# Attention over inducing points and a PReLU layer on one core: how the first batch is loaded and cast

## The chip, the cores and the metric

The kernel runs on one core of a Trainium2 chip. The metric is the device time of one execution in microseconds (us): the median of the runs given. Everything shown below of a profile is of one profiled execution, whose times are counted from the start of its span.

## The reference

`x` has 4 batches of 12480 rows of 128 numbers, `inducing` is 32x128. For each batch

```python
def mab(q, kv):
    s = (q @ kv.T) / sqrt(128)
    a = softmax(s)              # with 1e-9 added to the sum
    return a @ kv
h   = mab(inducing, x)          # 32 x 128, needs all of the batch's x
y   = mab(x, h)                 # 12480 x 128
hid = y @ w_in                  # 128 -> 2048
out = (maximum(hid, 0) + alpha * minimum(hid, 0)) @ w_out   # 2048 -> 128
```

All inputs and the output are f32 in device memory. So a batch has a first stage, which needs the whole batch and gives `h`, and a second one, which is work per row.

## The kernel before

**Tiles.** A batch is cut into six blocks of 2048 rows (16 tiles of 128 rows, one 128x2048 tile `xs` in f32 or `xn` in bf16) and a rest of 192 rows (`xn_left`). For the first batch `first_pieces` numbers them: piece 0 is block 0, piece 1 the rest, pieces 2 to 5 are blocks 1 to 4, pieces 6 and 7 are the two halves of block 5.

**First stage, for the first batch (the ramp).** Each piece is loaded as bf16 by a DMA that casts on its way (`a_load_cast`, L276 and L281, issued by POOL). Then TensorE transposes it in parts (`t` steps, L325), ScalarE or VectorE copy the parts out of the accumulators into `xT` (`c` steps, L331 and L333; a part is cut 0, 1 or 2 of a piece: 8, 4 and 4 tiles), TensorE multiplies by the inducing points (`s`, L340), VectorE takes the running minimum (`m`, L354 and L363), ScalarE the exponentials (`e`, L379, and the factors `f`, L397), TensorE transposes those (`u`, L417), they are copied out (`v`), TensorE multiplies them by `xn` (`h`, L434) and VectorE adds the result to a running sum (`g`, L448 and L450). A tail of small steps (`mg` to `hT`, L469 to L548) makes `h` of it.

What each engine does in the ramp is written out by hand in one string, `order`; each engine works through its own steps of it in that order. In a step the digit is the piece, the digit after the point the part, the last letter the engine (`a` ScalarE, `v` VectorE). `W4` means four matmuls on a tile of zeros (`warm`, L925, 512 columns each), whose result nobody reads.

**Second stage.** Its weights are loaded by POOL's queue too, behind the pieces: `w_in` cast to bf16 (`w_in_b`), `w_out` in f32. `w_in` is transposed by a DMA of SP's queue (`winT`, L1048). POOL multiplies `w_out` by `1 - alpha` (`weights`, tile `W`, L943) and by `alpha` (`linear_weights`, tile `AW`, L952), four instructions of 128x512 each; of the latter two come with the `weights` and two later, behind POOL's copy of `rep` (L1068). The work per row is then done in 416 visits: a visit multiplies four sets of 128 hidden units by 512 rows (L765), ScalarE or VectorE apply the relu (tile `gt`, L778 and L780), and one visit later TensorE multiplies by `W` (L791) into an accumulator, which is copied out (`ob`, L837, L844, L846) and stored by SP's queue. Four visits finish 512 rows, 16 visits a block.

**What else is in the visits.** The first stage of the next batch, and the softmax of the rows that come next, are laid into the visits by `at(visit, step)`. For batch 1 the pieces are loaded in f32 by SP (`a_load`, L290, into one of the four buffers of `xs_pool`), cast by POOL (`a_cast`, L308) and transposed by a DMA of SP's queue (`xT<-xn`, L317). The softmax of the rows of block 1 is in the list `when`: scores, maximum, difference (POOL, L683), exponential (ScalarE, L645), sums (POOL, L669), reciprocal (VectorE, L706), product (POOL, tile `rep`, L714) and a DMA transpose (`a<-rep`, L723). A planner (`Plan`) chooses for each relu and copy whether ScalarE or VectorE does it, from costs that are written in the code, before the program is built.

SP issues its DMAs in the order in which they stand. Each waits for the data that it needs, and for the DMA that held its completion semaphore before it (there are eight).

Of the kernel before, what the change touches and what calls it, by code (L numbers as in the profile page):

```python
# [21 lines left out]
P = 128  # L22
R = 4
ST = 16
# [6 lines left out]
def kernel(  # L31
# [9 lines left out]
    nc = tc.nc  # L41
# [3 lines left out]
    B, N, C = x.shape  # L45
# [218 lines left out]
        eng.memset(st.da[:], 0.0)  # L264
        return st

    def a_load_cast(st, pc):


        r0, nt, last = supers[pc.s]  # L270
        if pc.full:
            if pc.s not in st.xn:
                st.xn[pc.s] = xn_pool.tile([P, ST, C], bf16, name="xn", tag="xn")
            rows = x[st.b, r0 : r0 + nt * P, :].rearrange("(p j) c -> p j c", p=P)
            ts = slice(pc.t0, pc.t0 + pc.n)
            nc.gpsimd.dma_start(out=st.xn[pc.s][:, ts], in_=rows[:, ts])  # L276
        else:
            st.xn[pc.s] = xn_left
            for t in range(nt):
                n = last if t == nt - 1 else P  # L280
                nc.gpsimd.dma_start(  # L281
                    out=xn_left[:n, t, :], in_=x[st.b, r0 + t * P : r0 + t * P + n, :]
                )

    def a_load(st, pc):
        s = pc.s
        r0, nt, last = supers[s]
        if pc.full:
            st.xs[s] = xs_pool.tile([P, ST, C], f32, name="xs", tag="xs")
            nc.sync.dma_start(  # L290
                out=st.xs[s][:],
                in_=x[st.b, r0 : r0 + nt * P, :].rearrange("(p j) c -> p j c", p=P),
            )
        else:
            st.xs[s] = xs_left
            for t in range(nt):
                n = last if t == nt - 1 else P
                nc.sync.dma_start(
                    out=xs_left[:n, t, :], in_=x[st.b, r0 + t * P : r0 + t * P + n, :]
                )  # L300

    def a_cast(st, pc):
        s = pc.s
        r0, nt, last = supers[s]
        xs = st.xs[s]
        if pc.full:
            st.xn[s] = xn_pool.tile([P, ST, C], bf16, name="xn", tag="xn")
            nc.gpsimd.tensor_copy(out=st.xn[s][:], in_=xs[:])  # L308
        else:
            st.xn[s] = xn_left  # L310
            for t in range(nt):
                n = last if t == nt - 1 else P
                nc.gpsimd.tensor_copy(out=xn_left[:n, t, :], in_=xs[:n, t, :])

    def a_turn(st, pc):
        s, nt = pc.s, pc.n
# [544 lines left out]

    xn_left = const.tile([P, supers[-1][1], C], bf16, name="xn_left")
    e1T_left = const.tile([P, supers[-1][1] * P], bf16, name="e1T_left")
    blank = const.tile([P, 512], bf16, name="blank")
    for t in (xn_left, blank, e1T_left):
        nc.vector.memset(t[:], 0.0)
    st = new_state(0)
    for pc in first_pieces[:2]:
        a_load_cast(st, pc)
    ident32 = const.tile([P, P], f32, name="ident32")  # L870
    make_identity(nc, ident32[:])
    ind_f = const.tile([M, C], f32, name="ind_f")
# [9 lines left out]
    xs_left = const.tile([P, supers[-1][1], C], f32, name="xs_left")  # L882
    for pc in first_pieces[2:]:
        a_load_cast(st, pc)
# [36 lines left out]
    def warm(n):  # L921

        ps = sums(0)
        for _ in range(n):
            nc.tensor.matmul(ps[:], blank[:, :P], blank[:], start=True, stop=True)  # L925
# [12 lines left out]

    a2s = {}

    def weights(i, eng):
        ks = slice(i * R, (i + 1) * R)
        eng.tensor_tensor(  # L943
            out=W1[:, ks, :],
            in0=w_out_f[:, ks, :],
            in1=om_al[:, ks].unsqueeze(2).broadcast_to([P, R, C]),
            op=MULT,
        )

    def linear_weights(i):  # L950
        ks = slice(i * R, (i + 1) * R)
        nc.gpsimd.tensor_tensor(  # L952
            out=AW[:, ks, :],
            in0=w_out_f[:, ks, :],
            in1=alT[:, ks].unsqueeze(2).broadcast_to([P, R, C]),
            op=MULT,
        )
# [12 lines left out]
    kept = {}  # L970

    def first_products():
        b_products(st, 0, 0, BT)
# [5 lines left out]
    def first_less():  # L979
        kept["be"] = new_e()  # L980
        b_less(kept["b"], 0, BT, kept["bm"], kept["be"])

    def begin(step):


        if step[0] == "W":
            warm(int(step[1:]))
            return
        plain = {
            "mg": lambda: a_max(st),  # L990
            "rb": lambda: kept.update(rb=a_factors_pe(st)),
            "mm": lambda: a_factors_min(st, kept["rb"]),
            "mf": lambda: a_factors_exp(st),
            "ex": lambda: a_worth(st),
            "dn": lambda: a_total(st),
            "pd": lambda: kept.update(pd=a_den_pe(st)),
            "rec": lambda: a_den_rec(st, kept["pd"]),
            "ph": lambda: kept.update(ph=a_sum_pe(st)),
            "hT": lambda: a_sum_div(st, kept["ph"]),
            "b": first_products,  # L1000
            "bm": first_most,
            "bs": first_less,
            "be": lambda: b_exp_once(kept["be"], BT, w0[:, :BT]),
            "bt": lambda: kept.update(bt=b_turn_pe(w0[:, :BT], BT)),
            "ba": lambda: b_turn_copy(st, 0, 0, BT, kept["bt"], False),
            "b2": lambda: b_products(st, 0, BT, ST - BT, later),
            "w": lambda: a_w(st),
            "hw": lambda: a_w_copy(st),
            "hwv": lambda: a_w_copy(st, False),
        }  # L1010
        if step in plain:
            plain[step]()
            return
        f, act = step[0], step[-1] == "a"
        p, _, part = step[1:].rstrip("av").partition(".")
        pc = first_pieces[int(p)]
        if f in "tc":
            t0, n = cuts[pc.n][int(part)]
            if f == "t":
                kept["t", p, part] = a_turn_pe(st, pc, t0, n)  # L1020
            else:
                a_turn_copy(st, pc, t0, n, kept.pop(("t", p, part)), act)
        elif f == "u":
# [43 lines left out]
    def first_turn_dma():  # L1067
# [6 lines left out]
        for i in range(NV // 2, NV):  # L1074
            linear_weights(i)

    def first_sum():
        src = b_tree(w0, ST)
# [83 lines left out]
    for b in range(B - 1):  # L1162
# [90 lines left out]
```

## Time and profile before

| | |
|---|---|
| median of 3 runs (lowest, highest) | 601.41 us (600.49, 602.48) |
| time of the profiled execution | 601.52 us |
| its span, first to last instruction | 599.4 us |
| mean granted TensorE clock | 0.993 |
| PE, ACT, DVE, POOL busy | 98%, 91%, 87%, 36% of the span |
| first product of a visit (L765) starts at | 31.46 us |

The span is 2.1 us shorter than the execution's time; what lies around it is taken as fixed. The ramp is what stands ahead of 31.46 us, 5% of the span; the visits and the last stores take the rest.

### The profile page before, as it was taken

Reading aid. Unit: us, or ns where it says so; the run is one execution under the profiler, and the core shown is the slowest. Engines: PE = TensorE matmul, PEld = TensorE weight load, DVE = VectorE, ACT = ScalarE, POOL = GpSimd, SP = SyncE. Lnnn points to the kernel's source line nnn. Section 1 sums busy time; section 2 is a strip of 40 time slices with the busy share of each in tenths; the row PEclk is TensorE's granted clock in tenths of the full one; section 3 lists DMA queues with packets and bytes.
Section 4 is the critical chain, followed back from the end, with each engine's and each line's share of the span. In section 5 each row is a group of like instructions: output and inputs, shape, how many; then the busy total and the mean of one; then the engine's idle time right before and its main releaser. Section 6 shows DMA issues by size and latency. Waiting matters only on the chain.

```text
span 599.4 us, 22670 instructions
## 1 busy us (share of the span) xinstructions
PE 586.0 (98%) x9439; PEld 437.7 (73%) x9441; DVE 519.1 (87%) x944; ACT 546.8 (91%) x1110; POOL 214.3 (36%) x255
## 2 busy tenths in 40 slices
PE   7899999999999999999999999999999999999997
PEld 3567777777777777777777777777777777777775
DVE  5778988888998899988898889988899899899986
ACT  4679999999999999999999999999999999999996
POOL 4176535303416436233136155233133134144010
PEclk9899999999999999999999999999999999999999
DMA  8947999544178797641256999931242231442311
GB/s 163 212 149 158 211 199 221 106 91 73 55 188 188 224 221 177 108 99 54 73 127 204 189 197 238 169 81 55 72 77 68 73 90 54 115 74 68 90 57 58
DMA packets 122088, 76.81 MB, mean 128 GB/s; under 512 B 103953, under 2 KB 106113, under 8 KB 119681
## 3 DMA queue, kind: packets, MB, share of 16 engines
q1 hardware_dynamic: 120112, 70.50, 52.0%
q0 software_dynamic: 1648, 4.77, 4.0%
q8 instruction: 74, 1.21, 0.9%
q14 instruction: 30, 0.24, 0.2%
q10 hardware_dynamic: 224, 0.09, 0.1%
HBM read 28.07 MB, written 25.56 MB: 89 GB/s over the span
## 4 chain that ended last, share of the span: by engine, by line
PE 93%; DMA 4%; ACT 1%; issue 0%; DVE 0%; DVEq 0%; SPq 0%; ACTq 0%; POOLq 0%
PE bp L791 64%; PE hh L765 22%; DMA xn<-in_x_dram 3%; PE bp L818 2%; PE hh L601 2%; PE hh L434 1%; PE hh L340 1%; DMA a<-rep 1%; ACT gt L778 1%; PE hh L559 0%; PE hh L417 0%; PE bp L925 0%; DVEq L1248 0%; PE hh L325 0%; PE hh L482 0%
## 5 line engine op out<-in xcount | busy, mean ns | idle before, releaser
L778 ACT ACTIVATE gt<-hh 128x512 bf16<-128x512 f32 x887 | 471.1, 606 | 29.4 <-PE hh L765 20.5
L780 DVE TENSOR_SCALAR gt<-hh 128x512 bf16<-128x512 f32 x673 | 435.4, 685 | 51.3 <-PE hh L765 41.1
L791 PE MATMUL bp<-W,gt 128*128 128x128 bf16 x6240 | 416.6, 220 | 0.2 <-DVE gt L780 0.2
L791 PEld LDWEIGHTS <-gt 128*128 128x128 bf16 x6240 | 349.4, 98 | 85.7 <-issue 79.1
L765 PE MATMUL hh<-a,HW 32*128 32x512 bf16 (+2 forms) x1664 | 159.3, 371 | 1.9 <-ACT gt L778 1.3
L714 POOL TENSOR_TENSOR rep<-e,rc 128x2048 bf16<-128x2048 f32 (+1 forms) x24 | 84.5, 3520 | 19.1 <-DVE rc L706 19.1
L683 POOL TENSOR_TENSOR e<-e,smx 128x512 f32<-128x512 f32 (+1 forms) x24 | 24.6, 1025 | 169.9 <-DVE smx L678 169.9
L765 PEld LDWEIGHTS <-HW 32*128 32x128 bf16 x1664 | 41.0, 91 | 43.8 <-issue 7.3
L669 POOL TENSOR_TENSOR t<-e 128x256 f32<-128x256 f32 (+1 forms) x24 | 17.2, 716 | 131.3 <-ACT e L645 131.3
L844 ACT COPY ob<-bp 128x512 f32<-128x512 f32 (+1 forms) x63 | 37.1, 589 | 2.3 <-PE bp L791 1.4
L308 POOL CAST xn<-xs 128x2048 bf16<-128x2048 f32 x18 | 34.0, 1888 | 6.4 <-DMA xs<-in_x_dram 5.8
L669 POOL TENSOR_TENSOR t<-t 128x128 f32<-128x128 f32 (+3 forms) x100 | 30.3, 303 | 7.8
L354 DVE TENSOR_SCALAR_CACHE_REDUCE s<-hh 128x512 f32<-128x512 f32 (+2 forms) x29 | 18.1, 623 | 6.2 <-PE hh L340 5.9
L846 DVE COPY ob<-bp 128x512 f32<-128x512 f32 x31 | 21.1, 680 | 0.0
L379 ACT ACTIVATE e1T<-s,rm 128x512 bf16<-128x512 f32 (+1 forms) x25 | 17.7, 706 | 2.5 <-DVE rm L363 2.5
L818 PEld LDWEIGHTS <-a 32*128 32x128 bf16 x392 | 14.9, 93 | 6.3 <-issue 0.9
L818 PE MATMUL bp<-HA,a 32*128 32x128 bf16 x392 | 19.3, 215 | 0.0
L645 ACT ACTIVATE e<-e 128x512 f32<-128x512 f32 (+1 forms) x24 | 14.8, 615 | 1.3 <-POOL e L683 1.3
L678 DVE TENSOR_REDUCE smx<-e 128x16 f32<-128x512 f32 (+1 forms) x24 | 15.9, 662 | 0.0
L601 PE MATMUL hh<-hT,xT 128*128 128x32 bf16 x372 | 13.0, 177 | 0.4 <-DVE hT L548 0.4
L601 PEld LDWEIGHTS <-xT 128*128 128x128 bf16 x384 | 12.3, 96 | 0.9 <-issue 0.9
L659 ACT COPY e<-hh 128x512 f32<-128x512 f32 (+1 forms) x19 | 10.9, 573 | 2.0 <-PE hh L601 1.1
(110 smaller groups left out, 182.0 us busy)
## 6 DMA issues: line engine op xcount, KB each, us to landing
out_dram<-ob SPq DMA_DIRECT2D x97, 256.0 KB, 2.6
xs<-in_x_dram SPq DMA_DIRECT2D x18, 1024.0 KB, 5.9
xn<-in_x_dram POOLq DMA_DIRECT2D x5, 512.0 KB, 7.9
w_out_f<-in_moe_w_out_dram POOLq DMA_DIRECT2D x1, 1024.0 KB, 19.6
xn<-in_x_dram POOLq DMA_DIRECT2D x2, 256.0 KB, 14.0
w_in_b<-in_moe_w_in_dram POOLq DMA_DIRECT2D x1, 512.0 KB, 16.3
a<-rep SPq DMA_TRANSPOSE x25, 4.6
xT<-xn SPq DMA_TRANSPOSE x18, 6.2
```

What stands on the lines that cost most here:

```text
L308: nc.gpsimd.tensor_copy(out=st.xn[s][:], in_=xs[:])
L601: nc.tensor.matmul(ps[w, t, :], st.xT[:, tile0[s] + t, w], hTs[b][:], start=True, stop=True)
L669: nc.gpsimd.tensor_tensor(out=t[:, :n], in0=src[:, :n, :w], in1=src[:, :n, w : 2 * w], op=ADD)
L683: nc.gpsimd.tensor_tensor(out=st.e2[s][:, :n], in0=st.e2[s][:, :n], in1=st.m2[s][:, :n].unsqueeze(2).broadcast_to([P, n, M]), op=SUB,)
L714: nc.gpsimd.tensor_tensor(out=rep[:, :n], in0=st.e2[s][:, :n].unsqueeze(2).broadcast_to([P, n, R, M]), in1=rc[:, :n].unsqueeze(2).unsqueez ...
L765: nc.tensor.matmul(hh[:, q * cols + w.start : q * cols + w.stop], HWs[b][rows, v * P : (v + 1) * P], a2[rows, t0 : t0 + nt, :].rearrange(" ...
L778: nc.scalar.activation(out=gt[:, :cols], in_=hh[:, :cols], func=RELU)
L780: nc.vector.tensor_relu(gt[:, :cols], hh[:, :cols])
L791: nc.tensor.matmul(blk.acc[:, t * C : (t + 1) * C], gt[:, (q * nt + t) * P : (q * nt + t + 1) * P], W1[:, k, :], start=(not blk.begun), st ...
L818: nc.tensor.matmul(blk.acc[w, t * C : (t + 1) * C], blk.a2[rows, blk.t0 + t, w], HAs[b][rows, :], start=(not blk.begun and t == 0), stop=F ...
L844: nc.scalar.copy(out=ob[:, :nt], in_=acc)
L846: nc.vector.tensor_copy(out=ob[:, :nt], in_=acc)
```

## The change

- The ramp's pieces are loaded as f32 by SP's queue (`a_load`), five of them at the start. The others, `w_in` and `w_out`, are loaded by `load_next`: one after the last cast of each of blocks 0, 1, 2 and 3, whose buffers of `xs_pool` they take.
- The pieces are cast to bf16 in the parts in which they are transposed (`a_cast_part`, steps `k`), by POOL (`p`), ScalarE (`a`) or VectorE (`v`): thirteen part casts by POOL, and piece 1, five by ScalarE, one by VectorE. `w_in` is cast by POOL as a whole (`kwp`).
- `W` steps have 256 columns instead of 512, and there are more of them.
- `order` is written anew. The first four tiles' softmax no longer waits for the copy of `HW`, which ScalarE makes (`hw`) instead of VectorE (`hwv`).
- POOL makes three of the four `AW` products ahead of its copy of `rep`, one behind it.
- In the visits, `first_rec` comes one visit later, some steps of block 1's softmax one or two later, and the cast, transpose, scores and so on of batch 1's first two pieces four later.

```diff
-    def a_load_cast(st, pc):
...
-            nc.gpsimd.dma_start(out=st.xn[pc.s][:, ts], in_=rows[:, ts])
...
     def a_load(st, pc):
...
+            if s not in st.xs:
+                st.xs[s] = xs_pool.tile([P, ST, C], f32, name="xs", tag="xs")
+            rows = x[st.b, r0 : r0 + nt * P, :].rearrange("(p j) c -> p j c", p=P)
+            ts = slice(pc.t0, pc.t0 + pc.n)
+            nc.sync.dma_start(out=st.xs[s][:, ts], in_=rows[:, ts])
...
+    def a_cast_part(st, pc, t0, n, eng):
+        s = pc.s
+        if not pc.full:
+            a_cast(st, pc)
+            return
+        if s not in st.xn:
+            st.xn[s] = xn_pool.tile([P, ST, C], bf16, name="xn", tag="xn")
+        ts = slice(pc.t0 + t0, pc.t0 + t0 + n)
+        to, of = st.xn[s][:, ts], st.xs[s][:, ts]
+        if eng == "a":
+            nc.scalar.copy(out=to, in_=of)
+        else:
+            (nc.gpsimd if eng == "p" else nc.vector).tensor_copy(out=to, in_=of)
...
-    blank = const.tile([P, 512], bf16, name="blank")
+    blank = const.tile([P, 2 * P], bf16, name="blank")
...
-    for pc in first_pieces[:2]:
-        a_load_cast(st, pc)
+    for pc in first_pieces[:5]:
+        a_load(st, pc)
...
-    nc.gpsimd.dma_start(out=w_in_b[:], in_=moe_w_in)
-    w_out_f = xs_pool.tile([P, NK, C], f32, name="w_out_f", tag="xs")
-    nc.gpsimd.dma_start(out=w_out_f[:], in_=moe_w_out.rearrange("(k p) c -> p k c", p=P))
...
-    warm(7)
+    warm(14)
...
-    warm(4)
+    warm(9)
...
+    def load_next(done):
+        if not waiting:
+            return
+        what = waiting.pop(0)
+        if what == "w_in":
+            kept["w_in"] = xs_pool.tile([C, DFF], f32, name="w_in_f", tag="xs")
+            nc.sync.dma_start(out=kept["w_in"][:], in_=moe_w_in)
+        elif what == "w_out":
+            kept["w_out"] = xs_pool.tile([P, NK, C], f32, name="w_out_f", tag="xs")
+            nc.sync.dma_start(
+                out=kept["w_out"][:], in_=moe_w_out.rearrange("(k p) c -> p k c", p=P)
+            )
+        else:
+            for pc in what:
+                a_load(st, pc)
...
-        t0.1 t0.2 c0.2v t0.0 c0.0v c0.1a s0 t1.0 t2.0 m0 t2.2 c1.0v e0 t2.1 c2.2v c2.0v
-        s1 m1 e1 W4 t3.2 t3.0 f1 c3.2a c2.1v t3.1 c3.1a s2 u0 c3.0v u1 s3 v0a v1a t4.0
-        t4.1 m2 e2 t4.2 h0 h1 m3 c4.0v f3 c4.2a f2 c4.1v u2 g0 s4 g1 t5.2 v2v e3 c5.2a
-        t5.1 t5.0 c5.1a u3 m4 e4 c5.0v v3a t6.1 c6.1v h2 s5 t6.0 t7.1 g2 m5 t7.0 c6.0a
-        c7.1a c7.0v s6 m6 u4 h3 v4v e5 s7 e6 f4 m7 u5 u6 ex v5v h4 h5 mg g3 e7 rb f5 f6
-        u7 v6v g4 dn h6 mm v7a g5 mf h7 g6 f7 pd g7 rec ph hT W1 b w bm bs hwv b2 be W1
-        bt ba W2
+        k1.0p k0.2p k0.1p t0.2 k0.0v t0.0 c0.2v k2.1p k3.0p k3.2p t0.1 c0.0v c0.1v k2.2a
+        W8 t2.2 k2.0a k4.0p s0 t1.0 c2.2a c1.0a m0 W6 s1 t2.1 t2.0 k4.1p k3.1a m1 c2.1v
+        e0 t3.1 c2.0v c3.1v e1 W1 t3.0 c3.0a t3.2 f1 c3.2v k4.2a s2 W4 s3 m2 u0 u1 k5.0p
+        e2 k5.2p t4.2 m3 c4.2v t4.0 v0a v1a t4.1 u2 c4.0v h0 c4.1a v2v g0 f2 h1 k5.1a
+        k6.0p W2 s4 W1 t5.0 t5.2 t5.1 k6.1p k7.0p g1 e3 k7.1p m4 c5.0v f3 u3 c5.2a t6.0
+        c5.1v W3 s5 e4 t6.1 u4 v3a c6.0v m5 t7.0 c6.1a t7.1 v4a s6 f5 c7.0v h2 kwp c7.1v
+        W2 s7 m6 m7 e5 e6 mg h3 g2 f6 W2 u5 v5v f4 h4 u6 g3 rb e7 h5 u7 v6v h6 g4 ex mm
+        g5 f7 v7a W2 h7 mf dn pd g6 g7 rec W2 ph hT W3 b w bm bs be b2 W4 bt ba hw W5
...
+    waiting = [first_pieces[5:6], first_pieces[6:], "w_in", "w_out"]
...
-            for i in range(NV // 2):
+            for i in range(NV - 1):
                 linear_weights(i)
...
-    at(6, first_rec, cost=[("v", 160)])
+    at(7, first_rec, cost=[("v", 160)])
...
-            when = [1, 2, 3, 4, 5, 7, 8, 11]
+            when = [1, 2, 3, 5, 6, 9, 9, 11]
...
-            m = n + (8 * (p - 1) if p > 1 else p)
+            m = n + (8 * (p - 1) if p > 1 else p if b else p + 4)
```

More of the change, by code (lines that the diff above doesn't have):

```diff
@@ L265, in new_state @@
         return st
-    def a_load_cast(st, pc):
[L270 to L275, printed above, removed]
-            nc.gpsimd.dma_start(out=st.xn[pc.s][:, ts], in_=rows[:, ts])
[L277 to L283, printed above, removed]
     def a_load(st, pc):
@@ L288, in a_load @@
         if pc.full:
[L289 to L293, printed above, removed]
+            if s not in st.xs:
[3 more added lines that the diff above has]
+            nc.sync.dma_start(out=st.xs[s][:, ts], in_=rows[:, ts])
         else:
@@ L867 @@
     st = new_state(0)
-    for pc in first_pieces[:2]:
-        a_load_cast(st, pc)
+    xs_left = const.tile([P, supers[-1][1], C], f32, name="xs_left")
+    for pc in first_pieces[:5]:
+        a_load(st, pc)
     ident32 = const.tile([P, P], f32, name="ident32")
@@ L924, in warm @@
         for _ in range(n):
-            nc.tensor.matmul(ps[:], blank[:, :P], blank[:], start=True, stop=True)
-    warm(7)
+            nc.tensor.matmul(ps[:, : 2 * P], blank[:, :P], blank[:], start=True, stop=True)
+    warm(14)
     itp = ring([C, M], bf16)
@@ L939 @@
     a2s = {}
+    kept = {}
     def weights(i, eng):
@@ L944, in weights @@
             out=W1[:, ks, :],
-            in0=w_out_f[:, ks, :],
+            in0=kept["w_out"][:, ks, :],
             in1=om_al[:, ks].unsqueeze(2).broadcast_to([P, R, C]),
@@ L953, in linear_weights @@
             out=AW[:, ks, :],
-            in0=w_out_f[:, ks, :],
+            in0=kept["w_out"][:, ks, :],
             in1=alT[:, ks].unsqueeze(2).broadcast_to([P, R, C]),
@@ L1007, in begin @@
             "w": lambda: a_w(st),
+            "kwp": lambda: nc.gpsimd.tensor_copy(out=w_in_b[:], in_=kept["w_in"][:]),
             "hw": lambda: a_w_copy(st),
@@ L1014, in begin @@
         f, act = step[0], step[-1] == "a"
-        p, _, part = step[1:].rstrip("av").partition(".")
+        p, _, part = step[1:].rstrip("avp").partition(".")
         pc = first_pieces[int(p)]
@@ L1022, in begin @@
                 a_turn_copy(st, pc, t0, n, kept.pop(("t", p, part)), act)
+        elif f == "k":
+            a_cast_part(st, pc, *cuts[pc.n][int(part)], step[-1])
+            done = first_pieces[int(p)].s
+            if pc.full and step == last_cast[done]:
+                load_next(done)
         elif f == "u":
@@ L1036 @@
     order = """
-        t0.1 t0.2 c0.2v t0.0 c0.0v c0.1a s0 t1.0 t2.0 m0 t2.2 c1.0v e0 t2.1 c2.2v c2.0v
-        s1 m1 e1 W4 t3.2 t3.0 f1 c3.2a c2.1v t3.1 c3.1a s2 u0 c3.0v u1 s3 v0a v1a t4.0
-        t4.1 m2 e2 t4.2 h0 h1 m3 c4.0v f3 c4.2a f2 c4.1v u2 g0 s4 g1 t5.2 v2v e3 c5.2a
-        t5.1 t5.0 c5.1a u3 m4 e4 c5.0v v3a t6.1 c6.1v h2 s5 t6.0 t7.1 g2 m5 t7.0 c6.0a
-        c7.1a c7.0v s6 m6 u4 h3 v4v e5 s7 e6 f4 m7 u5 u6 ex v5v h4 h5 mg g3 e7 rb f5 f6
-        u7 v6v g4 dn h6 mm v7a g5 mf h7 g6 f7 pd g7 rec ph hT W1 b w bm bs hwv b2 be W1
-        bt ba W2
-    """
+        k1.0p k0.2p k0.1p t0.2 k0.0v t0.0 c0.2v k2.1p k3.0p k3.2p t0.1 c0.0v c0.1v k2.2a
[6 more added lines that the diff above has]
+        g5 f7 v7a W2 h7 mf dn pd g6 g7 rec W2 ph hT W3 b w bm bs be b2 W4 bt ba hw W5
+    """
+    waiting = [first_pieces[5:6], first_pieces[6:], "w_in", "w_out"]
+    last_cast = {}
+    for step in order.split():
+        if step[0] == "k" and step != "kwp":
+            last_cast[first_pieces[int(step[1])].s] = step
     for step in order.split():
@@ L1073, in first_turn_dma @@
         )
-        for i in range(NV // 2, NV):
-            linear_weights(i)
+        linear_weights(NV - 1)
     def first_sum():
```

4 lines of the change are left out of this document (removed).

## The prediction, made before the changed kernel ran

> **What bounds the kernel now.** First the page's chain of waits, then the same chain in order of time:
>
> ```profile
> PE 93%; DMA 4%; ACT 1%; issue 0%; DVE 0%; DVEq 0%; SPq 0%; ACTq 0%; POOLq 0%
> ```
>
> ```profile
> 1.25 5.33 DMA xn<-in_x_dram
> ...
> 6.86 14.41 DMA xn<-in_x_dram
> 21.32 1.03 PE hh L325 x8
> ```
>
> From 31.4 us on the chain is TensorE's own work, and no relayout of the ramp shortens that. Ahead of it, up to 21.3 us, the chain is the loads. The timeline shows how the pieces arrive and what follows the last:
>
> ```profile
> 9.64 1.07 PE L325 MATMUL hh<-ident,xn 128*128 128x128 bf16 x16 [0.55 <-DMA xn<-in_x_dram]
> 12.10 1.07 PE L325 MATMUL hh<-ident,xn 128*128 128x128 bf16 x16 [0.24 <-DMA xn<-in_x_dram]
> 14.56 1.07 PE L325 MATMUL hh<-ident,xn 128*128 128x128 bf16 x16 [0.29 <-DMA xn<-in_x_dram]
> 17.07 1.07 PE L325 MATMUL hh<-ident,xn 128*128 128x128 bf16 x16 [0.34 <-DMA xn<-in_x_dram]
> ...
> 21.32 1.03 PE L325 MATMUL hh<-ident,xn 128*128 128x128 bf16 x8 [0.66 <-DMA xn<-in_x_dram]
> ...
> 31.46 0.61 PE L765 MATMUL hh<-a,HW 32*128 32x512 bf16 x6
> ```
>
> Pieces 2 to 5 come 2.47 us apart (1.05 MB read each), piece 7 at 21.3; the visits start 9.1 us after its transposes end at 22.35. Eight transposes there take as long as sixteen before. The table by stretches says why:
>
> ```profile
> core 0: us, PE busy (x) PEld busy (x) DVE busy (x) ACT busy (x) POOL busy (x), PEclk, DMA share, GB/s
> 7.00:17.00 10.00, 7.71 (x111) 5.11 (x109) 7.74 (x24) 6.28 (x17) 2.11 (x3) 1.00 1.06 205
> 17.90:21.20 3.30, 1.74 (x37) 1.03 (x34) 2.22 (x6) 2.36 (x6) 0.00 (x0) 1.00 1.09 204
> 21.30:24.60 3.30, 3.28 (x42) 2.23 (x42) 1.88 (x8) 2.08 (x6) 0.00 (x0) 0.50 1.02 297
> 28.10:31.40 3.30, 3.06 (x39) 1.17 (x38) 1.83 (x5) 0.31 (x1) 3.30 (x4) 0.50 0.92 313
> 29.60:32.00 2.40, 2.40 (x25) 0.60 (x25) 0.81 (x3) 0.12 (x2) 2.40 (x4) 0.60 0.96 396
> ```
>
> In two stretches of the ramp the granted clock is half, each behind a stretch with a half-idle TensorE. The last row is one f32 load by SP's queue (batch 1's first) alone on the DMA engines: 396 GB/s, so 2.65 us for 1.05 MB. In the early visits one wait stands out:
>
> ```profile
> 40.46 0.63 ACT L645 ACTIVATE e<-e 128x512 f32<-128x512 f32 x1 [1.25 <-POOL e L683]
> 41.62 0.39 PE L765 MATMUL hh<-a,HW 32*128 32x512 bf16 x2 [0.84 <-ACT gt L778]
> ```
>
> POOL made two `AW` products (2.03 us, from 37.38) ahead of that difference; ScalarE stood behind it, and TensorE behind ScalarE's relus.
>
> **Part 1, the loads.** SP has nothing to wait for at the start; ScalarE's first DMA is issued at 0.75, so I take 0.7 for SP's. That first DMA, of 16 KB, lands 1.6 us after its issue. With 2.65 of data piece 0 lands at 0.7+1.6+2.65=5.0 (before: 6.6). The other bound is the least of the f32 loads' own landings, 5.2 after issue: 5.9. Piece 1 (96 KB) adds 0.25. Then four whole pieces and two halves, five times 2.65: pieces 2 to 7 land at 7.9, 10.5, 13.2, 15.8, 17.2 and 18.5, `w_in` at 21.1, `w_out` at 23.8. The later ones wait for casts: piece 5's load for piece 0's, done by 7, while the queue has data until 13.2; piece 6's for piece 2's, done by 9.5; `w_in`'s by 12. None of these waits ends last. Piece 7 gains 21.3-18.5=2.8 us.
>
> **Part 2, the casts.** POOL's 128x2048 cast takes 1.89 us, its 128x128 one 0.29; a line through both gives 0.61 for 512 and 1.04 for 1024. Piece 7 needs two in a row, ready at 18.5+1.22=19.75. POOL has 10 casts of 512, three of 1024 and piece 1's two (0.59): 9.8 us between 5 and 19.75, so it keeps up. ScalarE and VectorE are closer. ScalarE from piece 2's first part to the last copy of piece 6: ten 512-copies at 0.55 (0.59 in a row of two takes 1.13), two of 1024 taken as 1.0, two of 256 at 0.33, four exponentials at 0.74, a small one at 0.45, three factors at 0.2: 12.2 us, from 7.9 to 20.1, against 20.0 by the loads. VectorE by the same counting has 11.7 us from 5.0. Both are covered if they hardly wait; no rows show ScalarE or VectorE casting f32 from SBUF in this shape, and I take their PSUM copies' durations. VectorE's one cast (0.66 at that rate, 1.2 at half) is done before piece 2 lands, and costs nothing either way. The last transposes then end at 20.3, with 0.5 us for eight at full clock, against 22.35: 2.05 us gained.
>
> The page SBUF — State Buffer of the Trainium skill (section Who interferes with whom) says that POOL and VectorE block each other for a whole instruction when VectorE runs a copy or cast in its two-port mode, which would speak against casting on POOL. Here POOL's eight products of 128x512 took 1.033 to 1.039 us with VectorE's copies beside some and not others, and its 18 casts 1.881 to 1.891; only the one new SBUF cast of VectorE is of a kind that no row shows, and by the rule it would hold POOL for its 0.66 us, at piece 0.
>
> **Part 3, the clock and the tail.** `W` steps are added where TensorE waited: eight matmuls of 256 columns between the last transposes and `hT`, and twelve behind. I take the clock as full. That shortens what is TensorE's in the tail: the chain's five groups from 22.35 to 24.74 (2.38 us, about half of it array time, of which VectorE's and ScalarE's steps then hide most) 0.4; `rep`'s transposes 0.62 to 0.41 (the same sixteen at 35.79) 0.2; the last `W`, 1.03 us ahead of the first visit, to 0.54: 0.4, as the copy `a` was done at 31.03. The `hwv` copy leaves VectorE, whose `ba` waited for TensorE anyway: nothing. Sum 1.0. `W` (four at 1.04) starts at 23.8 and `AW` ends at 31.0; the first is needed at 30: hidden. The visits start at 31.46-2.05-1.0=28.4.
>
> A rule of the Trainium skill (TensorE: Matmul & The Clock Gate, Part 1) halves the clock after an idle window of about 3.4 us; by its words the added matmuls would buy nothing, as no wait was that long, and the sum would lack the 1.5 us of clock in Parts 2 and 3: 599.8. This trace disagrees: the longest wait of 17.9 to 21.2 was 1.2 us, and the clock halved.
>
> **Part 4, the early visits.** One `AW` product instead of two ahead of the difference, and the exponential a visit later: 0.84 of TensorE's wait and some 0.2 around it go. Against that, batch 1's first scores, maxima and `e` transposes now fall on visits 16 to 21, where block 1's outputs begin and `xs`'s next load stands in SP's queue. A VectorE step of 0.68 in the wrong place costs TensorE that much; the trace has no such row, so between 0 and two of them, 1.4. I take 0.8. SP's queue: block 2's `a<-rep` held TensorE for 0.40 us at 82.18, since a DMA transpose behind a load takes SP 5.6 to 6.3 us (1.9 otherwise). The small `e1T_left` transpose now stands behind that load, the large one behind it, and the load comes about a visit earlier: 0.4 as before, up to 2 if not. Net gain 0.2.
>
> **Sum.** 601.5 (its own execution; 0.1 above the median) less 3.05 and 0.2: 598.3.
>
> **Rivals.** (a) *The clock halves all the same.* For: full activity is not shown by any row for the new order. Against: `order` has 45 `W` matmuls of 256 columns where it had 8 of 512. Price: the 0.5 of Part 2, the 1.0 of Part 3 and 0.3 around them, 600.1. (b) *The three engines wait for each other.* ScalarE is busy 6.28 of 10.0 us and 2.36 of 3.3 (72%) in the two stretches above; in the changed ramp it needs nearly 100%. At 85% its 12.2 us take 14.4, the last copy comes 2.2 later, 600.5; at 72% they take 16.9, 4.8 later: 603.1. From 79% down it is slower than before. (c) *F32 to f32 loads at the pace of before's only one in the ramp, `w_out`*: `winT` was issued at 23.68, when `w_in` had landed, `W` started at 27.68, 4.0 us for 1.05 MB, 3.87 without the lead. Piece 7 then lands at 5.0+0.25+19.4=24.6, 6.1 later than in my sum: 604.4, slower. It decides above 3.3 us a piece (319 GB/s). Against it stands the 396 GB/s row; that row had the DMA engines to itself, as the new ramp has. (d) *Better*: the casting loads' 2.47 us also holds here (0.9) and Part 4 costs nothing (0.8): 596.6.
>
> **How the numbers follow.** The forecast has 0.62, its own range 597.0 to 599.5. (a) 0.10, (b) 0.14, (c) 0.08, (d) 0.06. The measurement tells 0.3%, 1.8 us, from no change. Faster: forecast, (d) and 0.04 of (b), 0.72. Same: (a) and 0.06 of (b), 0.16. Slower: (c) and 0.04 of (b), 0.12. The range goes from (d) to just above (a) and the middle of (b), 596.6 to 600.9.
>
> **What would show it.** In the changed profile: sixteen transposes about 2.65 us apart, the last at about 20 behind POOL's casts; granted clock 1.00 from 18 to 31; ScalarE over 90% busy from 8 to 20; first L765 near 28.4; no wait over 0.5 us behind `e` of L645; `a<-rep` at block 2 within 0.5 us. Transposes 3.3 us or more apart would make (c) right, loads done early with ScalarE's queue late (b), half clock (a). If the visits start at 28.4 and the time is not under 599.6, Part 4 was wrong.

## The result, and the profile after

| | before | changed |
|---|---|---|
| median (lowest, highest), 14 runs each, same chip | 601.23 us (599.39, 602.48) | 603.67 us (601.96, 605.32) |
| time of the profiled execution, its span | 601.52, 599.4 us | 601.96, 600.0 us |
| first product of a visit starts at | 31.46 us | 29.88 us |
| from there to the start of the last visit | 561.45 us | 563.78 us |

The changed kernel is slower: ratio 1.0042, 95% interval 1.0030 to 1.0054. Its profiled execution is its quickest one, 1.7 us under the median; so the trace below shows it at its best, and what it lacks is looked for in the experiments.

The page's chain of waits has hardly changed, since the visits carry it:

```profile
PE 93%; DMA 3%; ACT 1%; POOL 1%; issue 0%; DVE 0%; DVEq 0%; ACTq 0%
```

The same chain in order of time, up to the first pieces (start, length, what):

```profile
1.20 5.27 DMA al_f<-in_moe_alpha_dram
6.60 0.26 PE hh L923
6.86 2.03 PE bp L916 x9
8.89 1.40 PE hh L321 x16
10.29 0.87 PE bp L916 x8
```

The loads of `x` have left the chain. In their place stands an 8 KB load of ScalarE's queue (`alpha`, landed at 6.47 us instead of 2.81, now that the loads of `x` are issued ahead of it), and behind it TensorE never waits again until 24 us: part of what holds it there are the fillers (L916), nine of them for 2.03 us at half clock.

TensorE's timeline, with the transposes of pieces 4 and 5, the last part of piece 6, piece 7, and the first visit:

```profile
16.13 1.07 PE L321 MATMUL hh<-ident,xn 128*128 128x128 bf16 x16
18.58 1.06 PE L321 MATMUL hh<-ident,xn 128*128 128x128 bf16 x16
...
20.96 0.40 PE L321 MATMUL hh<-ident,xn 128*128 128x128 bf16 x4
...
21.41 0.73 PE L321 MATMUL hh<-ident,xn 128*128 128x128 bf16 x8
...
29.88 0.60 PE L761 MATMUL hh<-a,HW 32*128 32x512 bf16 x6
```

The last transposes end at 22.14 us; before it was 22.35. From there to the first visit it is 7.74 us, before 9.11. POOL's timeline shows what stands between the last data and those transposes:

```profile
16.82 1.60 POOL L309 CAST xn<-xs 128x1024 bf16<-128x1024 f32 x2 [0.91 <-DMA xs<-in_x_dram]
19.24 2.44 POOL L309 CAST xn<-xs 128x512 bf16<-128x512 f32 x4 [0.83 <-DMA xs<-in_x_dram]
```

Piece 6 landed at 19.19, piece 7 at 20.46 (before 21.27). Piece 6's two casts end as piece 7 lands, piece 7's start at 20.5 and end at 21.68, so POOL held nothing up here. The table by stretches, the same ones as before:

```profile
core 0: us, PE busy (x) PEld busy (x) DVE busy (x) ACT busy (x) POOL busy (x), PEclk, DMA share, GB/s
7.00:17.00 10.00, 9.99 (x113) 7.85 (x112) 8.19 (x23) 6.79 (x15) 5.40 (x10) 1.00 1.01 417
17.90:21.20 3.30, 3.27 (x43) 2.18 (x43) 2.95 (x10) 3.30 (x10) 2.37 (x5) 1.00 1.01 415
21.30:24.60 3.30, 3.30 (x82) 2.42 (x79) 3.09 (x14) 3.14 (x11) 1.88 (x2) 1.00 1.00 288
28.10:31.40 3.30, 2.84 (x50) 1.42 (x47) 1.76 (x6) 1.88 (x5) 3.30 (x4) 1.00 0.93 278
```

The clock is full from 18 us on, the loads move 415 to 417 GB/s, and TensorE is busy without a gap. Ahead of visit 7 the wait that stood out is gone (ScalarE's exponential, now at L641, follows two relus without a wait); visit 7 starts 3.45 us after visit 6 before, 2.22 us after. But TensorE's own waits from visit 6 to the end of block 2 (engine, line, releaser: us in total, times, longest) are now

```profile
PE hh L761 <- DMA a<-rep: 1.6, 1, 1.6
PE hh L336 <- DMA xT<-xn: 0.9, 1, 0.9
PE hh L336 <- DVE hs L446: 0.4, 1, 0.4
```

The starts of visits, changed less before, tell the story in one line: visit 0 -1.58, visit 7 -2.81, visit 15 -3.14, visit 16 -1.66, visit 23 -0.24, visit 31 +0.81, visit 36 +0.64, last +0.74. All of it, and more, is given back between visits 15 and 31. POOL and SP's queue say how:

```profile
46.32 3.61 POOL L710 TENSOR_TENSOR rep<-e,rc 128x2048 bf16<-128x2048 f32 x1 [3.39 <-PE hh L597]
49.88 1.89 POOL L290 CAST xn<-xs 128x2048 bf16<-128x2048 f32 x1
51.71 0.53 POOL L295 CAST xn_left<-xs_left 128x128 bf16<-128x128 f32 x2
```

```profile
49.96 1.82 SPq L719 DMA_TRANSPOSE a<-rep  x1
51.87 3.72 SPq L313 DMA_TRANSPOSE xT<-xn  x1
55.69 1.20 SPq L313 DMA_TRANSPOSE xT<-xn_left  x1
56.94 0.57 SPq L275 DMA_DIRECT2D xs<-in_x_dram  x1
58.08 5.55 SPq L313 DMA_TRANSPOSE xT<-xn  x1
```

POOL idles 3.39 us ahead of block 1's product. The row names a product of TensorE that ended then; what POOL needs is VectorE's reciprocal, which now comes at visit 9 and ends at 46.18 us; the cast of batch 1's first piece, which used to lie ahead of the product, comes behind it. So `rep` and the two transposes of `xT` reach SP's queue together: `a<-rep` lands 6.1 us after its issue (before 4.5), visit 16 waits 1.60 us for it, and behind these the next load and the next transpose are late too: 0.86 us at 67.3.

### The profile page after: what moved, and what is told of

Its sections match the earlier page's. It is cut to its first block, busy times and chain, and to the rows that moved or that the text cites. A ratio compares the mean times of both kernels' runs of the same rounds, so it can differ in the third digit from the quotient of the medians.

```text
span 600.0 us, 22789 instructions
## 1 busy us (share of the span) xinstructions
PE 589.0 (98%) x9490; PEld 442.5 (74%) x9490; DVE 520.1 (87%) x945; ACT 549.5 (92%) x1115; POOL 218.9 (36%) x260
## 4 chain that ended last, share of the span: by engine, by line
PE 93%; DMA 3%; ACT 1%; POOL 1%; issue 0%; DVE 0%; DVEq 0%; ACTq 0%
PE bp L787 62%; PE hh L761 21%; PE bp L814 2%; PE hh L597 2%; DMA xT<-xn 2%; PE hh L336 1%; PE hh L430 1%; PE bp L916 1%; PE hh L321 1%; DMA a<-rep 1%; DMA al_f<-in_moe_alpha_dram 1%; ACT gt L774 1%; POOL rep L710 1%; PE hh L413 0%; PE hh L555 0%
## 5 line engine op out<-in xcount | busy, mean ns | idle before, releaser
L814 PEld LDWEIGHTS <-a 32*128 32x128 bf16 x392 | 14.9, 93 | 6.7 <-issue 1.6
L641 ACT ACTIVATE e<-e 128x512 f32<-128x512 f32 (+1 forms) x24 | 14.8, 617 | 0.0
L916 PE MATMUL bp<-blank 128*128 128x256 bf16 x68 | 12.5, 323 | 1.2 <-DVE blank L862 1.2
```

The lines of the kernel that those rows point to most:

```text
L814: nc.tensor.matmul(blk.acc[w, t * C : (t + 1) * C], blk.a2[rows, blk.t0 + t, w], HAs[b][rows, :], start=(not blk.begun and t == 0), stop=F ...
```

## The experiments

Each kernel ran beside the kernel before on one chip, 12 times (e5 9, e6 7, e7 10 and e14 6 times). The four groups e1 to e4, e5 to e8, e9 to e12 and e13 to e15 ran on different chips, where the kernel before had medians of 601.18, 600.80, 600.97 and 600.97 us. "Visits" is the time from the first to the last visit's start less that of before (561.45 us), from the one profiled execution.

| kernel | median (range) us | ratio to before, 95% | visit 0 at | visits |
|---|---|---|---|---|
| e1_ramp_only | 601.91 (599.61–603.94) | 0.9997–1.0024 | 29.90 | +0.56 |
| e2_visits_only | 603.30 (600.51–605.94) | 1.0017–1.0055 | 31.37 | +3.48 |
| e3_pieces_back | 599.95 (598.81–601.95) | 0.9968–1.0003 | 31.68 | +0.08 |
| e4_rec_back | 600.74 (599.96–602.30) | 0.9991–1.0014 | 32.07 | +0.47 |
| e5_no_head_W | 603.71 (603.02–607.19) | 1.0026–1.0065 | 31.83 | +2.04 |
| e6_no_W | 603.86 (603.45–607.23) | 1.0033–1.0076 | 31.77 | +5.79 |
| e7_cast_loads | 602.14 (601.72–603.28) | 1.0000–1.0031 | 29.14 | +2.87 |
| e8_rec_pieces | 600.49 (599.45–602.33) | 0.9974–1.0004 | 29.91 | -0.43 |
| e9_cast_best | 599.51 (598.78–602.67) | 0.9959–0.9995 | 29.74 | +0.05 |
| e10_cast_no_W | 600.89 (600.09–606.27) | 0.9985–1.0029 | 31.10 | +5.10 |
| e11_before_early | 600.35 (599.12–601.30) | 0.9971–1.0002 | 30.62 | -0.59 |
| e12_cast_pieces | 598.89 (597.42–603.27) | 0.9944–0.9984 | 30.61 | -1.49 |
| e13_warm_first | 601.05 (598.74–603.22) | 0.9989–1.0016 | 31.08 | -0.01 |
| e14_after_warm_first | 604.46 (603.27–605.75) | 1.0045–1.0079 | 31.95 | +2.57 |
| e15_cast_no_nine | 598.83 (597.72–601.17) | 0.9960–0.9982 | 30.11 | -1.72 |

The profiled executions of e4, e6 and e10 are the longest of their runs, so their last two columns are not typical.

### The ramp alone, the visits alone, and each visit edit undone

e1 is the changed kernel with all three edits of the visits undone; e2 is the kernel before with only these:

```diff
-    at(6, first_rec, cost=[("v", 160)])
+    at(7, first_rec, cost=[("v", 160)])
-            when = [1, 2, 3, 4, 5, 7, 8, 11]
+            when = [1, 2, 3, 5, 6, 9, 9, 11]
-            m = n + (8 * (p - 1) if p > 1 else p)
+            m = n + (8 * (p - 1) if p > 1 else p if b else p + 4)
```

e3 undoes the last of the three only, in the changed kernel; e4 has `[1, 2, 3, 5, 6, 8, 8, 11]` there instead; e8 is both.

> The changed kernel with the steps in the visits put back where they were (first_rec at 6, block 1's list as before, batch 1's first two pieces not moved). Theory (the time is lost in visits 15 to 36, because the moved steps pile DMA transposes up in SP's queue): the ramp's 1.6 us and about 1 us of the early wait stay won, nothing is given back: 598 to 599.5 us, ratio 0.995 to 0.997, no wait of TensorE for a<-rep over 0.5 us. Rival (any earlier start of the visits runs into loads and transposes that can't come earlier): the gain is given back by visit 36, 600.5 to 602.

> The kernel before with only the moved steps in the visits (first_rec at 7, block 1's new list, batch 1's first two pieces four visits later). Theory: the early wait of 0.84 us behind POOL goes, then 2 to 4 us are lost in visits 15 to 36: 602.5 to 604.5. Rival (the ramp's earlier end is what makes the transposes late): 600 to 601.5, no loss.

> The changed kernel with batch 1's first two pieces back at their visits, block 1's new list kept. Theory: block 1's a<-rep still comes late (its reciprocal is at visit 9, and now two transposes of SP's queue may stand ahead of it), 1.5 to 3 us lost at visit 16; the later waits, up to visit 31, go: 601 to 603. Rival: all of the loss is the moved pieces': 598 to 599.5.

> The changed kernel with block 1's reciprocal and product at visit 8 instead of 9, all else as changed. Theory: rep is ready about 1.5 us earlier, the wait of 1.6 us for a<-rep at visit 16 shrinks under 0.5, part of it comes back at visit 22 and after (pieces' transposes wait behind the load): 602 to 603.3. Rival (the transposes of the pieces alone make it late, by sharing the DMA engines): no change from 603.7.

> The changed kernel with two of the visits' edits undone: batch 1's first two pieces four visits earlier, as before, and the reciprocal and product of block 1's softmax at visit 8 instead of 9. Kept are the third AW product ahead of rep, the first softmax's reciprocal a visit later, and the difference, exponential and sums' new visits. Theory: undoing the first alone gave 599.95 and the second alone 600.74; each takes away another wait behind visit 15 (the transposes of batch 1's first piece behind a load, and block 1's a behind VectorE's reciprocal), so both together keep the early visits' gain of 1.2 us and the ramp's: 598.3 to 599.8, faster than before by 0.2 to 0.5%. Rival (both are one queue's crowding, and either cure is enough): 599.7 to 600.8, no better than the better one alone.

The visits' edits alone cost 2.1 us (603.30 against 601.18 of their group), and either of two cures takes the loss away: pieces back 3.7 us of the changed kernel's median, reciprocal a visit earlier 2.9. Both together gain 3.2, no more than one alone: of e8's theories the rival held. So by the medians the two edits cost only together. (The medians of e3 and e4 came out below the ranges of their theories, that of e1 above its own.) In e1 POOL has the cast again where the changed kernel has its wait:

```profile
43.03 1.89 POOL L290 CAST xn<-xs 128x2048 bf16<-128x2048 f32 x1
44.86 0.53 POOL L295 CAST xn_left<-xs_left 128x128 bf16<-128x128 f32 x2
45.35 3.60 POOL L710 TENSOR_TENSOR rep<-e,rc 128x2048 bf16<-128x2048 f32 x1
```

and in e3, with the reciprocal still late, SP's queue has done the transposes of `xT` ahead of `a<-rep`, 4.6 us apart from it:

```profile
44.09 1.93 SPq L313 DMA_TRANSPOSE xT<-xn  x1
47.19 1.17 SPq L313 DMA_TRANSPOSE xT<-xn_left  x1
51.76 2.00 SPq L719 DMA_TRANSPOSE a<-rep  x1
```

The wait of 1.6 us for `a<-rep` at visit 16 is gone there. It is not gone in e1, which has the old visits: its `rep` is done at 48.95, but SP is busy with `xT<-xn_left` until 49.2 and with two output stores until 50.3. So the ramp alone came out at 601.91, no different from before, though in its profile the visits start 1.56 us earlier; how much of that is this wait was not tried by itself.

### The fillers

e5 leaves out `warm(9)` and the order's first `W8`, `W6`, `W1` and `W4`; e6 leaves out every `W` of the order:

```diff
-        W8 t2.2 k2.0a k4.0p s0 t1.0 c2.2a c1.0a m0 W6 s1 t2.1 t2.0 k4.1p k3.1a m1 c2.1v
+        t2.2 k2.0a k4.0p s0 t1.0 c2.2a c1.0a m0 s1 t2.1 t2.0 k4.1p k3.1a m1 c2.1v
```

> The changed kernel without the fillers between its first transposes: W8, W6, W1 and W4 of the order and the nine matmuls behind the transpose of alpha are left out; the later W steps stay. Theory: TensorE is busy without a gap from 6.8 to 24 us in the changed ramp, much of it at half clock, so these fillers stand on its path: without them TensorE waits for casts and loads again in the first pieces, piece 2's first transposes start up to 1 us earlier, the visits start at 29.0 to 30.0 whatever the clock does at the start, and the median is 601.5 to 603.0, up to 2 us below the changed kernel's. Rival (the fillers buy what they were put there for): the clock stays half behind the first pieces, piece 7's transposes and the tail are slower, the visits start at 31 or later, and the time is 604 to 606.

> The changed kernel without any W step of the order (the fourteen and nine matmuls on zeros ahead of the first piece stay). Theory: the fillers of the tail, from the last transposes on, stand beside waits of TensorE and keep its clock; without them the clock is half in a stretch between 22 and 30 us and the visits start 0.5 to 1.5 us later than in the kernel that lacks the first fillers only: 30 to 31.5, time 602.5 to 604.5. Rival (the fillers buy nothing, as no wait there is longer than some 1.2 us): visits start at 29.0 to 30.0 as without the first fillers, time within 0.5 us of that kernel's.

The theory that the first fillers stand on TensorE's path fell: without them the median is 603.71 against 603.67, and visit 0 comes at 31.83, with the clock half until 16.2 us. As far as the medians tell, what they take at half clock they give back by an earlier full one; the two were not measured apart. Nor do the 7 runs of e6 show that the later set is worth anything: 603.86 without any.

### The loads and the casts

e7 is the changed kernel, its order without the `k` steps, with the loads of before:

```diff
-    for pc in first_pieces[:5]:
-        a_load(st, pc)
+    for pc in first_pieces[:2]:
+        a_load_cast(st, pc)
...
+    for pc in first_pieces[2:]:
+        a_load_cast(st, pc)
+    nc.gpsimd.dma_start(out=w_in_b[:], in_=moe_w_in)
+    w_out_f = xs_pool.tile([P, NK, C], f32, name="w_out_f", tag="xs")
+    nc.gpsimd.dma_start(out=w_out_f[:], in_=moe_w_out.rearrange("(k p) c -> p k c", p=P))
```

> The changed kernel with its order, W steps and visits, but with the pieces, w_in and w_out loaded as in the kernel before, by POOL's casting DMAs, and without any k step. It measures the loads and casts by themselves. Theory (f32 loads gain little: pieces land 2.49 us apart against 2.47, piece 7 0.8 us earlier, and ScalarE's, POOL's and VectorE's casts are added): the visits start within 0.7 us of the changed kernel's 29.9, between 29.3 and 30.6, and the median is within 1.2 us of its 603.7. Rival (the loads carry the ramp's gain): the visits start at 31 or later, with the last transposes at 22 as before, and the median is 605 or more. Other rival (the casts cost more than the loads bring): visits start ahead of 29.2, median 602.3 or less.

The surprise: the edit that the change is named for is a loss, as the last of e7's theories had it. With the casting DMAs back the median falls by 1.5 us (by 1.1 if each is taken against the kernel before of its own group), and in the trace the visits start 0.74 us earlier than in the changed kernel's best execution. TensorE's timeline in e7 (piece 7, first visit):

```profile
20.72 0.61 PE L339 MATMUL hh<-ident,xn 128*128 128x128 bf16 x8
...
29.14 0.60 PE L779 MATMUL hh<-a,HW 32*128 32x512 bf16 x6
```

Piece 7 landed at 20.48 us there, as in the changed kernel (20.46); but it landed as bf16, and its transposes started 0.24 us later instead of 0.95. From their end to the first visit it is 7.8 us, as in the changed kernel. So in these profiles the gain of the ramp is that of the new order behind the last transposes, and it needs no f32 load.

The two corrections put together, and three kernels beside them:

- e9: e7 with the visits of e8. e12: e7 with the visits of e3.
- e10: e9 without any `W` in the order.
- e11: the kernel before, its own ramp, three `AW` products ahead of `rep`, and the visits of e8.

> The changed order with the loads of before (POOL's casting DMAs, no k step) and with the two visit edits undone that cost time: batch 1's first two pieces at before's visits, block 1's reciprocal and product at visit 8. Theory (the gain of the ramp is that of the new order, the f32 loads and casts on engines cost 1.5 us of it, and the late visits cost 3 us): the two corrections add up; visits start at 29.1, and the median is 600.5 - 1.5 = 599.0, between 598.2 and 599.8, faster than before by 0.2 to 0.5%. Rival (the two corrections overlap, as an earlier start only meets the same queue): 600.0 to 601.0, as the kernel with only the visits corrected.

> The kernel e9_cast_best without any W step in the order. Theory (the fillers are worth little, as two kernels with f32 loads and without fillers came out at 603.7 and 603.9 against 603.7 with them): visits start at 29 to 30, median within 0.7 us of e9_cast_best. Rival (with the casting loads TensorE has more waits, and the fillers carry the gain by keeping the clock full): clock half in one or two stretches between 17 and 31 us, as before, visits start at 30.5 to 31.5, median 1.3 to 2.3 us above e9_cast_best.

> The kernel before with its own ramp and loads, and only these edits: three AW products ahead of rep and one behind, block 1's difference, exponential and sums at the visits of the changed kernel, its reciprocal and product at visit 8, the first softmax's reciprocal a visit later. Theory: visit 7 comes 1.2 us earlier, as the difference no longer stands behind two AW products, and nothing gives it back: 599.6 to 600.4. Rival (a give-back at block 1's a or at the transposes of batch 1's pieces, as in the kernel with all visit edits): 601 to 602.5.

> The kernel e9_cast_best with block 1's reciprocal and product at visit 9, as in the changed kernel; only batch 1's pieces are put back. Theory (with the pieces back, SP's queue is free when rep comes, and the reciprocal's visit costs nothing: 599.95 with it at 9 and 600.49 with it at 8, with f32 loads): within 0.6 us of e9_cast_best. Rival (the late reciprocal costs by itself): 1.0 to 2.0 us above e9_cast_best, with a wait of 1 us or more for block 1's a at visit 16.

They add up, as expected: 599.51 against e8's 600.49, 598.89 against e3's 599.95. With the same visits the casting loads are better by 1.0, 1.1 and 1.5 us in three pairs, or by 1.2, 0.9 and 1.1 against the kernel before of each group. In each pair the two intervals overlap; it is that all three agree that carries this. e9 and e12 beat both kernels, e12 with the ratio 0.9964 (0.9944 to 0.9984); its TensorE has only these waits from 29 to 110 us:

```profile
PE hh L779 <- ACT gt L792: 0.5, 1, 0.5
PE hh L354 <- DMA xT<-xn: 0.2, 1, 0.2
```

e11 has the early visits alone, and its median is within its theory's range; but the theory said that nothing gives the gain back, and something does. Visit 7 comes 1.23 us sooner behind visit 6 than before, and at visit 9 TensorE loses 0.80 of it, as e11's waits of TensorE and its timeline of VectorE show:

```profile
PE bp L791 <- DVE ob L837: 0.8, 1, 0.8
45.79 0.25 DVE L706 RECIPROCAL rc<-den 128x16 f32<-128x16 f32 x1 [0.60 <-POOL den L693]
45.96 1.22 DVE L837 TENSOR_TENSOR ob<-bp,rec 128x512 f32<-128x512 f32 x2
```

With the reciprocal at visit 8, VectorE waits for POOL's sums ahead of the copies `ob`, and TensorE for those. e8 and e9, with the reciprocal at 8 too, lose 0.8 and 1.1 us there; e3 and e12, with it at 9, nothing. So once the pieces are back, the earlier reciprocal is no further cure. e9 against e11 is the new order against the old ramp with the same visits: 0.8 us by the medians, not clear of the noise.

Here the fillers do count: without them e10 is 1.4 us slower than e9, as the rival had it. Two stretches of its profile, with the columns of the table above:

```profile
7.00:17.00 10.00, 6.54 (x62) 4.45 (x59) 5.05 (x14) 3.46 (x8) 2.23 (x3) 0.69 1.05 204
28.10:31.40 3.30, 2.06 (x43) 1.34 (x45) 1.58 (x6) 0.78 (x2) 3.30 (x4) 0.98 1.16 280
```

TensorE is busy 65% of the first and the clock is 0.69 there; the half clock came from 10.8 to 17.6 us, ahead of where the rival looked for it, and again from 31.2.

### Casts, or the late start?

The chain of waits above names another culprit for the f32 loads' loss: `alpha` lands at 6.47 us, and TensorE idles from 5.1 to 6.6, where it warmed itself before. e13 (on e3) and e14 (on the changed kernel) fill that stretch; e15 empties it in e12, by leaving out the `warm(9)`:

```diff
+    warm(9)
     alp = ring([P, NK])
     nc.tensor.transpose(alp[:], al_f[:], ident32[:NK, :NK])
-    warm(9)
```

> The kernel e3_pieces_back with one move on TensorE: the nine matmuls on zeros stand ahead of the transpose of alpha instead of behind it. Theory of the late small load (with x on SP's queue from the start, alpha lands at 6.5 us instead of 2.8, TensorE idles from 5.1 to 6.6 where it warmed before, and the first pieces are transposed at half clock): the idle stretch is filled, the granted clock is full from 4 to 8 us on, the visits start at 29.0 to 29.9, and the median falls from 599.95 to between 598.4 and 599.3, what the casting loads gave with the same visits (598.9). Rival (the casts on the engines cost it, not the start): 599.5 to 600.4, no change.

> The changed kernel with the same one move: nine matmuls on zeros ahead of the transpose of alpha. Theory of the late small load: the median falls from 603.7 to between 602.1 and 602.8, what the casting loads gave with the same visits (602.1). Rival: 603.2 to 604.2, no change.

> The kernel e12_cast_pieces without the nine matmuls on zeros. Theory of the start (a TensorE that idles from 4.5 to 6.6 us loses the full clock for the first pieces): the kernel with casting loads loses what the f32 loads lost, median 599.6 to 600.6, visits' start 0.5 us or more later. Rival (the start's clock is given back by the time piece 7 lands): 598.5 to 599.4, no change.

The theory of the late start found no support in any of the three: filled, the kernels are 1.1 and 0.8 us slower, which is not clear of the noise, and not faster; emptied, the casting kernel is as fast as ever (598.83). e13's timeline shows the stretch filled, and behind it TensorE waiting for the casts:

```profile
5.07 1.16 PE L916 MATMUL bp<-blank 128*128 128x256 bf16 x9
6.56 0.20 PE L924 MATMUL hh<-ident,al_f 16*128 16x16 f32 x1 [0.33 <-DMA al_f<-in_moe_alpha_dram]
7.87 0.40 PE L321 MATMUL hh<-ident,xn 128*128 128x128 bf16 x4 [1.11 <-POOL xn L309]
9.05 1.25 PE L321 MATMUL hh<-ident,xn 128*128 128x128 bf16 x10 [0.79 <-DVE xn L309]
```

In e13 the full clock came at 5.0 us and was taken away at 8.4, as the first pieces were transposed; in e14 at 7.7, and for twice as long. So neither shows what a full clock for the first pieces would bring. In the changed kernel's profile it came at 9.8 and stayed. e4, whose ramp is the changed kernel's, lost it as e13 and e14 did; its stretches, cut where the clock may change:

```profile
core 0: us, PE busy (x) PEld busy (x) DVE busy (x) ACT busy (x) POOL busy (x), PEclk, DMA share, GB/s
4.65:8.06 3.41, 1.72 (x15) 1.25 (x15) 1.28 (x2) 0.43 (x2) 1.39 (x4) 1.00 1.01 389
8.06:11.48 3.42, 2.65 (x21) 2.17 (x19) 2.23 (x5) 1.56 (x2) 0.86 (x2) 0.50 1.01 422
11.48:14.89 3.41, 3.41 (x21) 1.82 (x18) 0.85 (x3) 1.98 (x4) 2.10 (x3) 0.50 1.01 425
```

TensorE is busy half of the first stretch, and the next two are at half clock. What it waits for in that stretch of e4 is not a cast but `alpha`:

```profile
6.50 0.20 PE L923 MATMUL hh<-ident,al_f 16*128 16x16 f32 x1 [1.37 <-DMA al_f<-in_moe_alpha_dram]
```

In e13 and e14, where that wait is filled, it is the first casts (1.11 and 1.13 us), and the clock goes all the same. e12, with the casting loads, lost it too, from 12.0 to 15.4 us, behind a wait of 1.69 us for a piece to land. So an early full clock was lost to any of the three waits, and no run shows it to be a cost of the engines' casts alone. What the profiles do show of the casts' loss of about 1 us is the 0.7 us by which a piece cast by an engine is transposed later than one that lands as bf16. How much the clock and the engines' 22 more instructions add was not measured by itself.

## Why the prediction was wrong

The profiled execution was to be 3.25 us shorter than before and is 0.44 longer; the median came 5.4 above the forecast. By the steps:

- **Part 1, the pace of the loads, held; their start and end did not.** Pieces 2 to 5 land 2.49 us apart, under the 2.65 taken, so rival (c) is out. But piece 0 landed at 6.29 instead of 5.0 (before 6.58): SP's loads are issued from 0.73, yet their first packets start at 1.76 and the first eight take 0.76 us each on average. And a 16 KB instruction fetch took 1.10 us from 16.73, behind which 15 of the 16 DMA engines had piece 7 at 19.32 and the last at 20.46. Such a fetch (0.95 us from 19.08) lies ahead of piece 7 in the kernel before too; it was in the 21.3 that the prediction started from, and not in its 18.5. Predicted 18.5, a gain of 2.8 us; it is 0.8. This is the step that failed in the ramp: the sum of the landings left out 1.3 us at the start and 1.1 at the end, of which the faster pace gave some 0.4 back.
- **Part 2, the casts, held.** Their durations were right (POOL 0.61 and 1.04 us, ScalarE 0.62 and 1.04), and from piece 7's landing to the end of its transposes it is 1.68 us, against 1.8. That the gain of 2.05 us at the last transposes became 0.21 is Part 1's late piece 7. The statement that VectorE's one cast "costs nothing either way" left out a cost of the other kind: `om_al`, 0.17 us before, took 1.34 beside POOL's casts of f32,

```profile
7.10 1.34 DVE L926 TENSOR_SCALAR om_al<-alT 128x16 f32<-128x16 f32 x1
```

  and held VectorE's cast until 8.36. It took 1.07 to 1.41 in all nine profiles with the engines' casts, and 0.17 to 0.31 in the eight without. In the changed profile TensorE was at its fillers then; in e13 it waited 0.79 us for that cast. That is the lock that the Trainium skill states (SBUF — State Buffer, section Who interferes with whom): my reading of POOL's products, which took the same time with VectorE's copies beside them or not, had told against it, and here the trace agrees with the page.
- **Part 3, the tail, held and was undersized:** 1.37 us between the last transposes and the first visit against 1.0, with the clock at 1.00 from 18 us on. Rival (a), which had the half clock at the last transposes and in the tail, is out in the changed profile. But the sum took the clock at the start as given. The same ramp's code started its visits at 29.88, 29.90, 29.91, 31.68 and 32.07 in five profiles (changed, e1, e8, e3, e4), with the clock full for good from 9.8, 9.8, 9.8, 12.6 and 14.9 us on. The loads do not explain these 2.2 us: in e4 piece 7 landed at 19.65, sooner than in the changed profile, and its transposes ended at 24.27 instead of 22.14. The range had no term for it. The changed profile is one of the lucky ones; how much of its 1.7 us under the median comes from that is not shown, as the other runs' ramps are not on record. The prediction also misread the second of the two half-clock stretches before: ahead of it TensorE was busy 2.72 of 3.30 us (24.7 to 28.0), not half idle.
- **Part 4, the early visits: the gain was right, the give-back was the largest miss.** The difference ahead of two `AW` products gave 1.23 us at visit 7 against 1.0. For the moved steps I took 0.8 and at most 1.4, as a VectorE step in the wrong place; and for SP's queue "0.4 as before, up to 2 if not". From visit 7 to the last it is +3.55 us. This is the step that failed in the visits, and the larger miss: the two were priced apart. I did not ask what POOL does while it waits for the later reciprocal, and the cast that could have filled its 3.39 us had been moved away by the other edit. By the medians of e3 and e4 either one alone costs about nothing, though in e4's profile, its longest run, 2.0 us are still lost from visit 15 to 31.
- **Rival (b)** is not borne out as put: ScalarE is busy 9.79 of the 12 us from 8 to 20, 82%, and 3.30 of 3.30 from 17.9 to 21.2, but the last transposes came behind POOL's casts. Its time of 603.1 is the nearest to the median, for another reason: the place that it names was no slower than before.

## What to carry to other kernels

A DMA that casts on its way is not slower here than an f32 load (2.47 against 2.49 us a piece), so an engine's cast is a pure addition at the end of the chain: keep the casting DMA where the last piece is waited for. When two moved steps share a queue, ask of each engine what now fills its wait, and try the moves together and each undone: here each alone was harmless by the medians, and both together cost about 3 us. The changed kernel was worth keeping once the loads of before were back and batch 1's pieces at their old visits: so it gives 598.9 us, 0.36% under the kernel before (0.16 to 0.56).

## What was not expected of the hardware

- In these profiles the clock changes on a grid of 3.41 us whose phase differs from run to run, and it is lost behind steps in which TensorE was busy too little, in most without a long gap. In the ramps, eight steps at full clock with TensorE busy for 1.83 us or less (0.54 to 1.83) were each followed by half; steps with 1.92 and more kept the full clock, but for the tail's small matmuls, where 2.00 to 2.74 were still followed by half in five profiles. In the visits 1.27, 1.51 and 1.52 were followed by half (e2, e6, e10), but 1.79 to 1.81 kept the full clock in four profiles (changed, e1, e5, e14). So busy time alone does not decide it, and what else does stays open. The longest wait in e4's step was 1.37 us. The Trainium skill (TensorE: Matmul & The Clock Gate, Part 1) has the same step of 3.4 us and says that it runs free of the kernel's start, so that the same kernel differs from run to run; the traces agree. Its condition for losing the clock, an idle window of that length, does not fit e4's step.
- Two small loads of ScalarE's queue, 16 and 8 KB, landed at 4.55 and 6.47 us in the changed profile, where SP's queue loads `x` from 0.73 us on, instead of 2.40 and 2.81.
- An instruction fetch of 16 KB took 0.88 to 1.61 us (74 in the changed profile). Behind the one of 1.10 us at 16.73 a whole piece landed 1.14 us after 15 of its 16 parts.
